# Gated sum of a Fourier mixer and a token MLP: Down's gathers without the gate and two PSUM banks at a time, five Fourier products as seven sub-products, the gate's rows in stage two

## The chip, the cores and the metric

The kernel runs on one core of a Trainium2 chip. The time is device microseconds of one execution. Before the change it is 1871.37 us, the median of 3 runs (1871.29 to 1871.44).

## What is computed

The input is `x` with S = 2048 tokens and D = 1024 channels, all in float32. Two blocks of it are mixed by a gate per token:

```python
a = einsum("bsd,ed->bse", x, dft_hid_re)            # A: a Fourier layer, real part
b = einsum("bsd,ed->bse", x, dft_hid_im)
A = einsum("ts,bse->bte", dft_seq_re, a) - einsum("ts,bse->bte", dft_seq_im, b)

h = layernorm(x)                                    # B: an MLP over the tokens, F = 3584
u = gelu(einsum("bsd,sf->bdf", h, w1) + b1)
B = (einsum("bdf,fs->bds", u, w2) + b2).transpose(0, 2, 1)

g = sigmoid((x * gate_w).sum(-1, keepdims=True))
out = g * A + (1 - g) * B
```

## The kernel before

**Four stages.** Each is one large matrix product, and they run one after the other on TensorE: *Fourier* (names with q; the sequence transform, 2048 x 2048 for the cosine and for the sine, times x, written to DRAM as `q`), *Up* (u; w1 times the normalised rows `h`, then gelu, written as `u`), *Mixed* (y; the hidden transform of `q`, times the gate, into the output) and *Down* (o; w2 times `u`, times one minus the gate, added onto the output).

**26 block products per stage.** A stage is a bilinear scheme (`SCHEME`): the matrices are cut into 4 x 4 by 4 x 2 blocks, and 26 products of sums of blocks give what 32 products of blocks would. For each product VectorE (DVE) adds or subtracts blocks (L606, L609), sums that are used again being kept or stored and loaded again; ScalarE (ACT) then rounds an operand to a high part (L636), DVE makes the low part (L643, or L641 with the sign turned), and TensorE multiplies high x high, high x low and low x high (L948 to L950). A product has 96 matmuls of 128x128 by 128x512 in Fourier (4 row blocks m, 2 column halves n, 4 k), 84 in Up (7 m, 4 k), 48 in Mixed (4 m, 4 k) and 84 in Down (4 m, 7 k). One product of Fourier, number 24 of the scheme, is itself made as seven sub-products of 12 matmuls (`strassen`, L1097), named in `Q_INNER`: sums of its quarters are called s and t, its direct quarters a and b, and it adds up some results inside PSUM (L606 on `ps_q_p`).

**Gathers.** A finished product is read out of PSUM once for each block of the result that it belongs to, by a copy if it is the first (L1008, or in Down L1403 on ACT and L1405 on DVE), else by a fused multiply and add on DVE (L1016). Products that follow each other with nearly the same result blocks are chained: the next goes on accumulating in the same banks, and only differences are read. A block that is complete goes to DRAM (L622); if it returns after a gap of more than `Q_GAP` products it is stored and later loaded again or added by an accumulating DMA (L1268 in Fourier). In Down a block is added onto the output by an accumulating DMA of GpSimd (L1445); the blocks that end in the last product are loaded first and stored by SyncE (SP).

**PSUM.** It is four slots of two banks each (`SLOTS["pp"]`). Fourier, Up and Mixed take a slot for two neighbouring m at once and read both with one instruction of 128x1024 (Up's seventh m alone). Down has `together = False`: it takes single banks, halves of a slot, and a half that comes free beside a used half is given out before a free slot is opened. Down's reads are 128x512 and multiply by the gate of their 128 rows (`hgate` or `ngate`, one column of it per row block).

**Gate.** The row products of x with `gate_w` (L1525, sixteen of 128x1024 on DVE into `zg`) are made where the rows for Up are loaded and normalised, at the end of Fourier and the start of Up. The gate itself is made in Up's product 10.

**Order.** All work is listed as tasks with a due place. `Graph.schedule` plays them through by a table of costs and writes down one fixed order for each engine: DVE, ACT, the DMA queue of SP (loads) and the one of POOL (stores and accumulating DMAs). `RESERVE` and `Store.fits` say how many slots are kept for tasks that are due earlier. The engines follow that order and wait on semaphores.

Of the kernel before, what the change touches and what calls it, by code (L numbers as in the profile page):

```python
# [26 lines left out]
RESERVE = 7  # L27
# [81 lines left out]
Q_ORDER = [5, 14, 23, 3, 7, 11, 21, 22, 18, 24, 6, 17, 0, 13, 9, 8, 19, 15, 12, 2, 20, 25, 1, 16, 10, 4]  # L109
# [31 lines left out]
Q_GAP = 8  # L141
Q_DMA = {}
Q_INNER = (24,)
# [69 lines left out]
SUMS_AT, SUMS_STEP = ("q", 4), 2.5  # L213
SQUARES_AT, SQUARES_STEP = ("q", 12), 2
GATES_AT = "u", 10
H_LEAD, H_EACH = 8, 0.6
# [49 lines left out]
class Buf:  # L266
    def __init__(self, kind, name, t=None, parts=1, dtype=F32):
        self.kind, self.name, self.t, self.parts, self.dtype = kind, name, t, parts, dtype
        self.writer = [None] * parts
        self.readers = [[] for _ in range(parts)]  # L270
        self.taker = None
        self.users, self.opens = set(), False
        self.lane = dtype if kind == "h" else kind


class View:
    def __init__(self, buf, c0, n, part=None):
        self.buf, self.c0, self.n, self.part = buf, c0, n, part

    @property  # L280
    def ap(self):
        return self.buf.t[:, self.c0:self.c0 + self.n]
# [52 lines left out]
class Store:  # L335
# [6 lines left out]
    def pairs(self, ahead, kinds):  # L342
        return sum((max(0, ahead[d] - len(self.part[d])) + 1) // 2 for d in kinds)

    def fits(self, b, ahead):
        if b.kind == "f":
            return len(self.free["f"]) > ahead["f"]
        if b.kind == "h":
            if len(self.part[b.dtype]) > ahead[b.dtype]:
                return True  # L350
            return len(self.free["f"]) + len(self.free["h"]) > ahead["f"] + self.pairs(ahead, (F32, F32R))
        if b.kind == "ps" and len(self.part["ps"]) > ahead["ps"]:
            return True
        return len(self.free["pp"]) > ahead["pp"] + self.pairs(ahead, ("ps",))
# [30 lines left out]
class Graph:  # L385
# [63 lines left out]
    def schedule(self):  # L449
# [25 lines left out]
        def has_slots(t):  # L475
            if not all(b.engine for b in t.behind):
                return False
            for b in t.need:
                if not store.fits(b, {k: min(bisect_left(waiting[k], t), RESERVE) for k in waiting}):
# [3 lines left out]
        def start(t, e):  # L483
# [8 lines left out]
            if t.nbytes:  # L492
# [3 lines left out]
                idle[e] = max(idle[e], lanes[e].pop(0))  # L496
            heapq.heappush(events, idle[e])
# [7 lines left out]
        while events:  # L505
# [13 lines left out]
            if idle["PE"] <= now and at < len(pe) and not left[pe[at]] and has_slots(pe[at]):  # L519
                start(pe[at], "PE")  # L520
                at += 1
            for e, heap in ready.items():
                held = []
                while heap and idle[e] <= now and len(held) < 60:
# [3 lines left out]
                    if has_slots(t):  # L528
# [11 lines left out]
def gated_mix_kernel(  # L540
# [84 lines left out]
    def split(key, v, name, negate=False, pair=False):  # L625

        if pair:
# [82 lines left out]
    class Bilinear:  # L710
# [11 lines left out]
        halved = ()  # L722
        together = True
        ahead = 3

        def __init__(self, name, nk, nm, nn, wn, rn, big, keep, order, extra, perm):
# [19 lines left out]
            self.C, self.PS, self.half = {}, {}, {}  # L746
# [16 lines left out]
            for q in range(8):  # L763
                at = [j for j, r in enumerate(self.reads) if q in dict(r)]
                b = perm[0][q // 2] * 2 + perm[2][q % 2]
                self.ends[b] = [i for i, nxt in zip(at, at[1:] + [999]) if nxt - i > self.gap]
# [20 lines left out]
        def during(self, j, key):  # L787
# [10 lines left out]
            if (self.name, j) == GATES_AT:  # L798
                assert len(self.h) == NS
                gates(key)  # L800
# [46 lines left out]
        def operand(self, x, j, k, key):  # L847
# [34 lines left out]
            v, sv, _ = self.term(x, e, last, j, k, key)  # L882
            return v, s * sv

        def build(self):
            nonlocal step
            factor = [1] * self.chains
            for j in range(len(self.out)):
# [5 lines left out]
                for ks in self.groups(j):  # L894
# [21 lines left out]
                    for k in ks:  # L916
                        parts = {}
                        for x in "RW":
# [9 lines left out]
                            parts[x] = [View(h.buf, h.c0 + at, self.n[x], h.part) for h in pair[u]]  # L928
# [4 lines left out]
        def split(self, x, key, v, j, k, negate):  # L933
            return split(key, v, f"{self.name}_p{j}_{x.lower()}_{self.label(k)}", negate, self.pairs and v.n == H)
# [21 lines left out]

        def banks(self, j):
# [11 lines left out]
        def take(self, key, j, m, n, eps):  # L969

            bank, at = self.PS[j % self.chains, m, n], [(m, n)]
            if bank.buf.kind == "pp":
# [4 lines left out]
            for q, coef in self.reads[j]:  # L977
# [10 lines left out]
                if new and not back:  # L988
# [31 lines left out]
    class Fourier(Bilinear):  # L1020
        wide = Q_WIDE
        behind = Q_BEHIND
        halved = Q_INNER
        gap = Q_GAP
        takes = Q_TAKES

        def __init__(self):
            super().__init__("q", 4, 4, 2, H, D, "R", {"R": 1, "W": 2}, Q_ORDER, Q_SUMS, Q_PERM)

        def by_dma(self, x_, j, k, o):  # L1030
            return x_ == "R" and j > 1 and k in Q_DMA.get(Q_ORDER[j], ())
# [231 lines left out]
        def finish(self, key, b, m, n, o, j):  # L1263
            dst, reg = self.place(b, m, n)
            if j == self.ends[b][0] or self.back(b, j):
# [99 lines left out]
    class Down(Bilinear):  # L1365
# [6 lines left out]
        together = False  # L1372
# [24 lines left out]

        def copy(self, key, b, m, n, o, ps, coef):
# [206 lines left out]
```

## Time and profile before

| | |
|---|---|
| median of 3 runs | 1871.37 us |
| the profiled execution | 1871.47 us, span 1869.7 us |
| granted TensorE clock | 1.000 |
| DMA | 473.20 MB, 253 GB/s; queue of SP 369.19 MB, of POOL 102.26 MB |
| HBM | 367.81 MB read, 103.81 MB written |

Line numbers are those of the kernel before. In the profile's groups stands line, engine, operation, output <- inputs, shape and count, then busy time, mean duration in ns, and the idle time of the engine just before these instructions with what ended it. PE is TensorE, PEld its weight loads, SPq the queue of SP. In the windows each engine has its busy time and, in brackets, its instructions. How the time lies over the stages is read in the prediction.

### The profile page before, as it was taken

To read this page: it belongs to the slowest core of one execution; us is meant where nothing else is said; L and a number is where in the kernel's file an instruction comes from. 1 tells how busy PE (TensorE), PEld (TensorE's weight loads), DVE (VectorE), ACT (ScalarE), POOL (GpSimd) and SP (SyncE) were. 2 spreads that over 40 slices of the span, in tenths; PEclk is the share of its full clock that TensorE was granted. 3 is DMA by queue.
4 is the path that set the end of the run, shared out by engine and by line. 5 is a ranking of instruction groups with operands and counts; after the bars stand their busy time and mean duration, and the time that the engine had idled before them with its cause. 6 is when DMAs were issued, how large, how long until landed. Compare 5 with 4: busy or idle time off the path is not lost.

```text
span 1869.7 us, 23585 instructions
## 1 busy us (share of the span) xinstructions
PE 1848.6 (99%) x8118; PEld 1519.9 (81%) x8118; DVE 1688.5 (90%) x2091; ACT 873.4 (47%) x1210; POOL 200.7 (11%) x346
## 2 busy tenths in 40 slices
PE   9999999999999999999999999999999999999999
PEld 7888888888888888888888888788887778778887
DVE  8899779979979989696979999999999998889995
ACT  5445436643466434343535654454654344444441
POOL 0100010021021120001101200010310010001101
PEclk9999999999999999999999999999999999999999
DMA  9977679889697766366675988587997564675963
GB/s 379 387 262 277 223 279 364 316 293 392 231 326 266 252 231 234 127 231 203 224 251 209 373 280 261 194 273 285 326 338 238 182 207 158 186 203 119 300 178 68
DMA packets 187303, 473.20 MB, mean 253 GB/s; under 512 B 22768, under 2 KB 23536, under 8 KB 187184
## 3 DMA queue, kind: packets, MB, share of 16 engines
q1 hardware_dynamic: 154224, 369.19, 57.4%
q0 software_dynamic: 32672, 102.26, 16.7%
q8 instruction: 63, 1.03, 0.2%
q14 instruction: 56, 0.46, 0.1%
q10 hardware_dynamic: 288, 0.26, 0.0%
HBM read 367.81 MB, written 103.81 MB: 252 GB/s over the span
## 4 chain that ended last, share of the span: by engine, by line
PE 86%; DVE 8%; DMA 3%; issue 1%; ACT 1%; SPq 0%; DVEq 0%; ACTq 0%
PE ps_o_p L948 9%; PE ps_u_p L949 9%; PE ps_u_p L948 9%; PE ps_u_p L950 9%; PE ps_q_p L950 9%; PE ps_q_p L948 9%; PE ps_q_p L949 9%; PE ps_o_p L950 9%; PE ps_o_p L949 9%; PE ps_y_p L948 2%; PE ps_y_p L950 2%; PE ps_y_p L949 2%; DVE y_c L1016 1%; PE ps_q_p L1097 1%; DVE o_c L1016 1%
## 5 line engine op out<-in xcount | busy, mean ns | idle before, releaser
L950 PE MATMUL ps_q_p<-q_p_r_hi,q_p_w_lo 128*128 128x512 f32 x784 | 305.2, 389 | 0.9 <-DVE q_p_w_lo L641 0.8
L949 PE MATMUL ps_q_p<-q_p_r_lo,q_p_w_hi 128*128 128x512 f32 x784 | 305.0, 389 | 0.0
L948 PE MATMUL ps_q_p<-q_p_r_hi,q_p_w_hi 128*128 128x512 f32 x784 | 305.0, 389 | 0.0
L948 PE MATMUL ps_o_p<-o_p_r,o_p_w 128*128 128x512 f32 x726 | 284.7, 392 | 13.3 <-DVE o_c L1016 11.3
L949 PE MATMUL ps_o_p<-o_p_r,o_p_w 128*128 128x512 f32 x726 | 282.6, 389 | 0.0
L950 PE MATMUL ps_o_p<-o_p_r,o_p_w 128*128 128x512 f32 x726 | 282.6, 389 | 0.0
L949 PE MATMUL ps_u_p<-u_p_r_lo,u_p_w_hi 128*128 128x512 f32 x518 | 201.5, 389 | 0.0
L948 PEld LDWEIGHTS ps_o_p<-o_p_r,o_p_w 128*128 128x128 f32 x726 | 136.2, 188 | 49.3 <-DVE o_c L1016 13.1
L636 ACT ACTIVATE q_p_r_hi<-q_R_p 128x1024 fp32r<-128x1024 f32 (+1 forms) x96 | 100.4, 1053 | 160.2 <-DVE q_R_p L606 78.9
L950 PEld LDWEIGHTS ps_q_p<-q_p_r_hi,q_p_w_lo 128*128 128x128 f32 x784 | 147.1, 188 | 32.4 <-DVE q_p_w_lo L641 1.7
L949 PEld LDWEIGHTS ps_q_p<-q_p_r_lo,q_p_w_hi 128*128 128x128 f32 x784 | 147.1, 188 | 30.7
L948 PEld LDWEIGHTS ps_q_p<-q_p_r_hi,q_p_w_hi 128*128 128x128 f32 x784 | 147.2, 188 | 30.2
L950 PEld LDWEIGHTS ps_o_p<-o_p_r,o_p_w 128*128 128x128 f32 x726 | 136.3, 188 | 28.5
L949 PEld LDWEIGHTS ps_o_p<-o_p_r,o_p_w 128*128 128x128 f32 x726 | 136.3, 188 | 27.7
L636 ACT ACTIVATE u_p_w_hi<-u_W_p 128x896 fp32r<-128x896 f32 x104 | 97.4, 949 | 128.1 <-DVE u_W_p L606 68.3
L948 PE MATMUL ps_u_p<-u_p_r_hi,u_p_w_hi 128*128 128x512 f32 x385 | 149.8, 389 | 0.0
L950 PE MATMUL ps_u_p<-u_p_r_hi,u_p_w_lo 128*128 128x512 f32 x385 | 149.8, 389 | 0.0
L948 PE MATMUL ps_u_p<-u_p_r_lo,u_p_w_hi 128*128 128x512 f32 x343 | 133.4, 389 | 0.0
L950 PE MATMUL ps_u_p<-u_p_r_lo,u_p_w_lo 128*128 128x512 f32 x343 | 133.4, 389 | 0.0
L643 DVE TENSOR_TENSOR q_p_r_lo<-q_R_p,q_p_r_hi 128x1024 fp32r<-128x1024 f32 (+1 forms) x96 | 115.5, 1217 | 9.6 <-ACT q_p_r_hi L636 5.9
L1016 DVE SCALAR_TENSOR_TENSOR q_c<-ps_q_p,q_c 128x1024 f32<-128x1024 f32 x84 | 101.1, 1222 | 23.1 <-PE ps_q_p L950 20.2
L949 PEld LDWEIGHTS ps_u_p<-u_p_r_lo,u_p_w_hi 128*128 128x128 f32 x518 | 97.2, 188 | 20.2
(414 smaller groups left out, 3738.9 us busy)
## 6 DMA issues: line engine op xcount, KB each, us to landing
q_R_p<-in_ct_dram SPq DMA_DIRECT2D x131, 512.0 KB, 8.1
u_W_p<-in_w_dram SPq DMA_DIRECT2D x120, 448.0 KB, 5.0
o_W_p<-in_w_dram SPq DMA_DIRECT2D x94, 256.0 KB, 5.3
q<-q_c POOLq DMA_DIRECT2D x80, 256.0 KB, 6.8
q_W_p<-in_x_dram SPq DMA_DIRECT2D x77, 256.0 KB, 8.4
u<-u_c POOLq DMA_DIRECT2D x74, 256.0 KB, 4.5
y_W_p<-q SPq DMA_DIRECT2D x72, 256.0 KB, 5.6
y_R_p<-in_dt_dram SPq DMA_DIRECT2D x53, 256.0 KB, 5.9
```

The lines of the kernel that those rows point to most:

```text
L636: g.add({"ACT": act(v.n)}, key, lambda e: nc.scalar.activation(hi.ap, v.ap, AF.Copy, scale=-1.0 if negate else 1.0), r=(v.reg,), w=(hi.reg,))
L643: nc.vector.tensor_sub(lo.ap, v.ap, hi.ap.bitcast(F32))
L948: nc.tensor.matmul(bank.ap, wh.ap[:, c], rh.ap[:, e], start=a, stop=False, skip_group_check=True)
L949: nc.tensor.matmul(bank.ap, wh.ap[:, c], rl.ap[:, e], start=False, stop=False, skip_group_check=True)
L950: nc.tensor.matmul(bank.ap, wl.ap[:, c], rh.ap[:, e], start=False, stop=b, skip_group_check=True)
L1016: lambda e: nc.vector.scalar_tensor_tensor(o.ap, ps.ap, scale, o.ap, op0=ALU.mult, op1=ALU.add),
L1097: nc.tensor.matmul(bank.ap, l, r, start=start and k == i == 0, stop=done and k == 1 and i == 2, skip_group_check=True)
```

## The change

It does five things.

1. `Q_INNER` names five products of the scheme (1, 4, 15, 17, 24) instead of one: four more products of Fourier are made as seven sub-products.
2. Down takes PSUM in pairs of banks (`together = False` goes) and its copies and fused adds no longer multiply by the gate; a finished block is multiplied once, by ACT, ahead of its accumulating DMA. Blocks that are added onto the loaded output (those that end in the last product) are still read bank by bank, with the gate. In the last product, two banks have a slot each.
3. The row products of the gate leave `normalise` and have loads of their own in Up (`row_gates`, from product 4 on, one row for every three steps); the gate is made behind them.
4. Fourier's tables: other sums are kept (`Q_XR`, `Q_KEEP`), some sums of R blocks are made by an accumulating load (`Q_DMA`), a gap for each block (`Q_GAP`), and a block that returns is always added by an accumulating DMA. `Q_ORDER` swaps two neighbours, and the squares start at product 16.
5. The planner reserves 6 slots instead of 7, and does not let ACT or DVE start on a PSUM slot that the other is still reading.

```diff
-RESERVE = 7
+RESERVE = 6
...
-Q_ORDER = [5, 14, 23, 3, 7, 11, 21, 22, 18, 24, 6, 17, 0, 13, 9, 8, 19, 15, 12, 2, 20, 25, 1, 16, 10, 4]
+Q_ORDER = [5, 14, 23, 3, 7, 11, 21, 22, 18, 24, 6, 17, 0, 13, 9, 8, 19, 15, 12, 2, 25, 20, 1, 16, 10, 4]
...
-Q_GAP = 8
-Q_DMA = {}
-Q_INNER = (24,)
+Q_GAP = (12, 3, 12, 6, 12, 12, 1, 3)
+Q_KEEP = (2, 2)
+Q_INPLACE = ""
...
+Q_DMA = {10: (0, 2, 10), 24: (2, 10), 2: (1, 2), 16: (3, 10, 12), 19: (3, 12), 23: (1, 2, 3), 17: (0, 1, 3, 10, 12), 15: (0, 1), 20: (10,), 21: (3, 10), 13: (0, 2), 0: (3, 12), 3: (0, 2), 22: (10,), 14: (10,), 8: (10, 12), 6: (0,), 9: (1,), 18: (12,), 4: (3,), 5: (0,)}
...
+Q_INNER = (1, 4, 15, 17, 24)
...
-SQUARES_AT, SQUARES_STEP = ("q", 12), 2
-GATES_AT = "u", 10
-H_LEAD, H_EACH = 8, 0.6
+SQUARES_AT = ('q', 16)
+SQUARES_STEP = 2
+GATES_AT = "u", 4
+GATES_STEP = 3
+H_LEAD = 5
+H_EACH = 0.6
...
+            if e != "PE" and any(b.kind in ("ps", "pp") and b.reader not in (None, e) and b.until > now for b in t.bufs):
+                return False
...
             bank, at = self.PS[j % self.chains, m, n], [(m, n)]
-            if bank.buf.kind == "pp":
+            if bank.part is not None:
...
-                if new and not back:
+                if len(at) > 1 and self.single(b, j):
+                    for i, (one, part) in enumerate(zip(at, os)):
+                        self.accumulate(key, b, *one, part, View(bank.buf, i * H, H, i), eps * coef)
+                elif new and not back:
                     self.copy(key, b, m, n, o, bank, eps * coef)
...
-            if j == self.ends[b][0] or self.back(b, j):
+            if j == self.ends[b][0] or (b, m, n) in self.brought:
                 store(key, dst, reg, o)
...
-        together = False
...
+        def single(self, b, j):
+            return self.back(b, j)
+
+        def banks(self, j):
+            super().banks(j)
+            if j == len(self.out) - 1:
+                for m in (2, 3):
+                    self.PS[j % self.chains, m, 0] = View(Buf("pp", f"ps_o_p{j}_{m}_0", None, 4), 0, H)
+
         def copy(self, key, b, m, n, o, ps, coef):
-            i, t = (b // 2) * 4 + m, hgate if coef > 0 else ngate
...
+            plain_copy(key, o, ps, float(coef))
 
         def accumulate(self, key, b, m, n, o, ps, coef):
+            if not self.back(b, self.reading):
+                return fused(key, o, ps, float(coef))
             i, t = (b // 2) * 4 + m, hgate if coef > 0 else ngate
             fused(key, o, ps, t.t[:, i:i + 1], (t,))
...
-                g.add({"POOL": ISSUE["POOL"]}, key, lambda e: nc.gpsimd.dma_start(dst, o.ap, accum_op=ALU.add),
+                g.add({"ACT": act(H) + 0.08}, key, lambda e: nc.scalar.activation(
+                    o.ap, o.ap, AF.Copy, scale=hgate.t[:, i:i + 1]), r=(o.reg, hgate), w=(o.reg,))
+                g.add({"POOL": ISSUE["POOL"]}, key + 0.5, lambda e: nc.gpsimd.dma_start(dst, o.ap, accum_op=ALU.add),
...
-    def normalise(k, v, key):
-
-        col, junk = slice(k, k + 1), slot(D, f"z{k}")
+    def row_gates(k, key):
+        v, col = slot(D, f"x{k}_g"), slice(k, k + 1)
+        if GW.buf.taker is None:
+            load(key, GW, bass.AP(tensor=gate_w.tensor, offset=gate_w.offset, ap=[[0, P], [1, D]]))
         load(key, v, x[k * P:(k + 1) * P, :])
...
-            junk.ap, v.ap, 1.0, GW.ap, op0=ALU.mult, op1=ALU.mult, accum_out=zg.t[:, col]),
+            v.ap, v.ap, 1.0, GW.ap, op0=ALU.mult, op1=ALU.mult, accum_out=zg.t[:, col]),
```

How this moves instructions shows at three places.

The first is PE in Down, at the end of the sixth product (p5, its last k) and the start of the seventh (p6). A PSUM slot is named by the tile that opened it: `ps_o_p4_2_0` is the slot of banks m = 2 and 3, opened by the fifth product and still used by the chained sixth. Before:

```order
L949 MATMUL ps_o_p4_2_0_11532<-o_p5_r_6_11567,o_p5_w_6_11573 128x512
L950 MATMUL ps_o_p4_2_0_11532<-o_p5_r_6_11567,o_p5_w_6_11573 128x512
L948 MATMUL ps_o_p4_2_0_11532<-o_p6_r_0_11596,o_p6_w_0_11561 128x512
L949 MATMUL ps_o_p4_2_0_11532<-o_p6_r_0_11596,o_p6_w_0_11561 128x512
L950 MATMUL ps_o_p4_2_0_11532<-o_p6_r_0_11596,o_p6_w_0_11561 128x512
```

And the same place now:

```order
L974 MATMUL ps_o_p4_2_0_11687<-o_p5_r_6_11716,o_p5_w_6_11722 128x512
L975 MATMUL ps_o_p4_2_0_11687<-o_p5_r_6_11716,o_p5_w_6_11722 128x512
L973 MATMUL ps_o_p6_0_0_11977<-o_p6_r_0_11747,o_p6_w_0_11725 128x512
L974 MATMUL ps_o_p6_0_0_11977<-o_p6_r_0_11747,o_p6_w_0_11725 128x512
L975 MATMUL ps_o_p6_0_0_11977<-o_p6_r_0_11747,o_p6_w_0_11725 128x512
```

Before, the seventh product's first bank is a half of the slot that the sixth product has just left; now it is in a slot opened for it.

The second is DVE at the same boundary, where it reads the sixth product into a block (`o_c5`). Before:

```order
L1016 SCALAR_TENSOR_TENSOR o_c5_0_10966<-ps_o_p4_0_0_11509,ngate_77,o_c5_0_10966 128x512
L641 SCALAR_TENSOR_TENSOR o_p7_w_2_11787<-o_W11_p2_0_10818,o_p7_w_2_11787 128x512
L1016 SCALAR_TENSOR_TENSOR o_c5_0_10966<-ps_o_p4_0_0_11509,ngate_77,o_c5_0_10966 128x512
L609 TENSOR_TENSOR o_W3_p1_5_10766<-o_W3_p1_5_10766,o_R2_p1_1_10570 128x512
L1016 SCALAR_TENSOR_TENSOR o_c5_2_10991<-ps_o_p4_2_0_11532,ngate_77,o_c5_2_10991 128x512
L609 TENSOR_TENSOR o_R3_p0_6_10513<-o_R3_p0_6_10513,y_W0_p3_0_8416 128x512
L1016 SCALAR_TENSOR_TENSOR o_c5_2_10991<-ps_o_p4_2_0_11532,ngate_77,o_c5_2_10991 128x512
```

Now:

```order
L1048 SCALAR_TENSOR_TENSOR o_c5_0_11143<-ps_o_p4_0_0_11663,o_c5_0_11143 128x1024
L622 TENSOR_TENSOR u_Rs16_1_7835<-u_Rs16_1_7835,o_R2_p1_2_10789 128x512
L622 TENSOR_TENSOR o_W11_p2_0_10985<-o_W11_p2_0_10985,y_R4_p4_1_8660 128x512
L1048 SCALAR_TENSOR_TENSOR o_c5_2_11166<-ps_o_p4_2_0_11687,o_c5_2_11166 128x1024
L661 TENSOR_TENSOR o_p7_r_3_11989<-u_c1_6_5307,o_p7_r_3_11989 128x512
```

Four reads of one bank with the gate became two of two banks without it.

The third is DVE in Fourier at the twelfth product (p11; number 17 of the scheme), one of the four that change their form. Before, it makes the low parts of the operands while it reads an earlier product:

```order
L643 TENSOR_TENSOR q_p11_w_0_1_lo_2003<-q_W7_p10_0_1_1791,q_p11_w_0_1_hi_1918 128x1024
L643 TENSOR_TENSOR q_p11_r_0_lo_2014<-q_R28_p10_0_1718,q_p11_r_0_hi_2001 128x1024
L643 TENSOR_TENSOR q_p11_r_1_lo_2026<-q_R28_p10_1_1772,q_p11_r_1_hi_2011 128x1024
L606 TENSOR_TENSOR q_R28_p10_2_1855<-q_R28_p10_2_1855,q_R11_p11_2_1940 128x1024
L1016 SCALAR_TENSOR_TENSOR q_c1_0_1094<-ps_q_p9_0_0_1814,q_c1_0_1094 128x1024
L606 TENSOR_TENSOR q_R28_p10_3_1871<-q_R28_p10_3_1871,q_R11_p11_3_1943 128x1024
L643 TENSOR_TENSOR q_p11_r_2_lo_2060<-q_R28_p10_2_1855,q_p11_r_2_hi_2051 128x1024
```

Now the sums t and s, their splits and the sums inside PSUM stand there (ten rows of it):

```order
L625 TENSOR_TENSOR q_p11_t3_2174<-q_R28_p10_2_1638,q_R9_p9_0_1476 128x512
L625 TENSOR_TENSOR q_p11_t3_2174<-q_R28_p10_3_1724,q_R28_p10_1_1553 128x512
L625 TENSOR_TENSOR q_p11_s3_2181<-q_W7_p10_0_1_1567 128x512
L1042 TENSOR_SCALAR q_p11_p5_2193<-ps_q_p11_2_1_2155 128x1024
L661 TENSOR_TENSOR q_p11_t3_lo_2208<-q_p11_t3_2174,q_p11_t3_hi_2189 128x1024
L661 TENSOR_TENSOR q_p11_s3_lo_2219<-q_p11_s3_2181,q_p11_s4_hi_2179 128x512
L622 TENSOR_TENSOR ps_q_p11_0_1_2221<-ps_q_p11_2_0_2127,q_p11_p5_2193 128x1024
L661 TENSOR_TENSOR q_p11_s3_lo_2219<-q_p11_s_1992,q_p11_s4_hi_2179 128x512
L661 TENSOR_TENSOR q_p11_t4_lo_2236<-q_p11_t_1931,q_p11_t4_hi_2166 128x1024
L1048 SCALAR_TENSOR_TENSOR q_c5_0_402<-ps_q_p11_0_0_2162,q_c5_0_402 128x1024
```

Short sums and splits of 128x512 took the place of splits of 128x1024, and they stand among the product's own reads. Over the whole program PE has 8080 matmuls instead of 8128, DVE 2099 instructions instead of 2077.

90 lines of the change are left out of this document (54 added, 36 removed).

## Prediction

> **What bounds the kernel now.** I read the page's head and its chain first, to see which engine carries the span.
>
> ```profile
> span 1869.7 us, 23585 instructions
> PE 1848.6 (99%) x8118; PEld 1519.9 (81%) x8118; DVE 1688.5 (90%) x2091; ACT 873.4 (47%) x1210; POOL 200.7 (11%) x346
> PEclk9999999999999999999999999999999999999999
> PE 86%; DVE 8%; DMA 3%; issue 1%; ACT 1%; SPq 0%; DVEq 0%; ACTq 0%
> ```
>
> TensorE is 99% busy at full clock and has 86% of the chain, so time is won in two ways only: fewer matmuls, or fewer gaps between them. A matmul's record overlaps the next one, so its price is not the mean of a group but the distance between starts. The chain of waits has one piece that gives it:
>
> ```profile
> 202.11 19.04 PE ps_q_p L1097 x84
> ```
>
> 84 matmuls in 19.04 us without a break: 0.2267 us each. This piece is also the one block product of Fourier that is already made as seven sub-products. Next, the gaps stage by stage, from the first matmul of each stage in the timeline of PE:
>
> ```profile
> 4.03 0.80 PE L1241 MATMUL ps_q_p<-q_p_r_hi,q_p_w_hi 128*128 128x256 f32 x2
> 569.58 0.39 PE L948 MATMUL ps_u_p<-u_p_r_hi,u_p_w_hi 128*128 128x512 f32 x1
> 1064.62 0.39 PE L948 MATMUL ps_y_p<-y_p_r,y_p_w 128*128 128x512 f32 x1
> 1350.87 0.39 PE L948 MATMUL ps_o_p<-o_p_r,o_p_w 128*128 128x512 f32 x1
> 1863.55 1.59 PE L1432 MATMUL ps_o_p<-o_p_r,o_p_w 128*128 128x256 f32 x12
> ```
>
> The program has 25 x 96 + 84 = 2484 matmuls of full width in Fourier, 26 x 84 = 2184 in Up, 26 x 48 = 1248 in Mixed and 26 x 84 - 6 = 2178 in Down before the last line. At 0.2267 us these are 563.0, 495.0, 282.9 and 493.7 us. The stages took 565.6, 495.0, 286.3 and 512.7. **Lost between matmuls: 2.5 in Fourier, 0 in Up, 3.4 in Mixed, 19.0 in Down.** The groups of the page agree on whom the stage waits for (their idle column is smaller, since an ending record covers 0.16 us of each gap):
>
> ```profile
> L948 PE MATMUL ps_o_p<-o_p_r,o_p_w 128*128 128x512 f32 x726 | 284.7, 392 | 13.3 <-DVE o_c L1016 11.3
> L948 PE MATMUL ps_y_p<-y_p_r,y_p_w 128*128 128x512 f32 x208 | 81.7, 393 | 1.5 <-DVE y_c L1016 1.4
> ```
>
> In Down it is the read of a PSUM bank by L1016. One such place, after the sixth product, in the timelines of PE, ACT and DVE:
>
> ```profile
> 1467.72 0.39 PE L950 MATMUL ps_o_p<-o_p_r,o_p_w 128*128 128x512 f32 x1
> 1468.21 0.69 ACT L1403 ACTIVATE o_c<-ps_o_p,hgate 128x512 f32<-128x512 f32 x1 [0.52 <-PE ps_o_p L950]
> 1468.99 0.74 DVE L1016 SCALAR_TENSOR_TENSOR o_c<-ps_o_p,ngate,o_c 128x512 f32<-128x512 f32 x1
> 1469.79 0.50 PE L948 MATMUL ps_o_p<-o_p_r,o_p_w 128*128 128x512 f32 x1 [1.67 <-DVE o_c L1016]
> 1471.05 0.40 PE L950 MATMUL ps_o_p<-o_p_r,o_p_w 128*128 128x512 f32 x1
> 1471.48 0.69 ACT L1403 ACTIVATE o_c<-ps_o_p,hgate 128x512 f32<-128x512 f32 x1 [2.58 <-PE ps_o_p L950]
> 1472.20 0.75 DVE L1016 SCALAR_TENSOR_TENSOR o_c<-ps_o_p,ngate,o_c 128x512 f32<-128x512 f32 x1 [1.87 <-ACT o_c L1403]
> 1473.01 0.50 PE L948 MATMUL ps_o_p<-o_p_r,o_p_w 128*128 128x512 f32 x1 [1.57 <-DVE o_c L1016]
> ```
>
> Six matmuls run between two waits of 1.84 and 1.73 us (the distances 2.07 and 1.96, less 0.23). By the order of PE (the first place shown with the change) these six are the first bank of the next product, and it lies in the slot whose two banks ACT and DVE are just reading: it waits for the read of the old half, and the read at 1471.48 in turn waits until the six are done. Mixed, which takes its banks two at a time and so whole slots, loses 3.4 us over as many products.
>
> **The change, part by part.** *Matmuls.* Four more products of Fourier go from 96 to 84: 48 x 0.2267 = **10.9 us** off PE. The other stages keep their counts.
>
> *Down's banks.* Banks are taken in pairs, each in a slot of its own; in the order the seventh product starts in another slot than the one being read. What remains is a chained product, which goes on in the same banks: its first pair is complete when the second pair's 12 matmuls (2.72 us) begin, and these are what the reads have to fit behind.
>
> ```profile
> 1172.05 2.28 DVE y_c L1016 x2
> L1016 DVE SCALAR_TENSOR_TENSOR o_c<-ps_o_p,ngate,o_c 128x512 f32<-128x512 f32 x52 | 38.9, 749 | 24.6 <-PE ps_o_p L950 21.5 <-ACT o_c L1403 2.7
> ```
>
> Two reads of a pair are 2.28 us on DVE, under 2.72, so even a pair read twice is free just in time. Mixed does exactly this over as many products, with DVE fuller than Down's: its 3.4 us is the nearest row, and I take it. **Down: 19.0 to 3.4, 15.6 us off**; the ends are 0 left and 19.0 left. The gate now comes once per finished block, 28 times, on ACT (like the next row), which is idle more than half of the stage, and the accumulating DMA behind it has a whole product of 19 us; cost 0. Without that cover each would put 0.8 us before a DMA whose block nothing in Down reads again.
>
> ```profile
> L1307 ACT ACTIVATE y_c<-y_c,biases,gate 128x512 f32<-128x512 f32 x32 | 23.8, 807 | 18.1 <-DVE y_c L1016 18.0
> ```
>
> *DVE in Fourier.* Seven sub-products need sums and splits of their own. Counted in the order of DVE, Fourier gets 76 more instructions of 128x512 (32 for t, 16 for s, 20 folded splits, 8 of b) and 9 fewer of 128x1024 (16 + 8 splits, 15 sums of R and 8 reads go; 16 + 8 + 4 splits, 8 sums and 2 copies in PSUM come). Back to back they cost 0.60 and 1.14:
>
> ```profile
> 1201.00 1.20 DVE y_p_w L641 x2
> 1202.20 1.14 DVE y_R_p L606
> core 0: us, PE busy (x) PEld busy (x) DVE busy (x) ACT busy (x) POOL busy (x), PEclk, DMA share, GB/s
> 0.00:569.00 569.00, 567.33 (x2494) 467.52 (x2495) 501.05 (x477) 281.55 (x326) 56.66 (x104) 1.00 0.85 312
> 569.00:1064.00 495.00, 495.00 (x2186) 409.87 (x2185) 436.51 (x510) 226.90 (x305) 63.99 (x119) 1.00 0.67 230
> 1064.00:1350.00 286.00, 284.47 (x1249) 233.23 (x1248) 283.63 (x350) 149.37 (x208) 32.35 (x61) 1.00 0.80 273
> 1350.00:1870.00 520.00, 501.83 (x2195) 409.26 (x2193) 467.31 (x757) 215.56 (x373) 47.73 (x63) 1.00 0.67 200
> 400.00:500.00 100.00, 100.00 (x443) 82.77 (x442) 95.36 (x93) 38.66 (x41) 10.72 (x20) 1.00 0.82 312
> 0.00:569.00 569.00, 14.52 (x24) 1.00 0.85 312
> ```
>
> That is 76 x 0.60 - 9 x 1.14 = 35.3 us more. The gate's 16 row products (L1525, the last row, 14.52 us of them in this stage) go to Up. So DVE has 501 + 35 - 15 = 521 of 558 us, 93%. The window 400 to 500 shows DVE at 95% and PE without a gap, and the sub-products at 202 had none; Mixed, with DVE at 99%, lost 3.4 in 286, which over 558 us would be 6.6. I take 1 us, with the ends 0 and 6.6. Up gets the 15 us and reaches 451 of 495, below the same window: 0.
>
> *Gate rows.* Their loads (16 of 512 KB, with the gate's row) join Up, where DMA is at 0.67 of its time and PE never waits; one more ACT table load there. SP's queue issues 1058 DMAs in all instead of 1073, so nothing is pushed back on it. Cost 0, and if Up's cover were gone some 1.3 us for the table.
>
> *DMA in Fourier.* 112 stores of q instead of 80, 48 of them accumulating instead of 8; 15 loads of R add onto a tile by DMA; 8 reloads of q, and some of R, go. The bytes stay near 312 x 569 = 177 MB; the accumulated part is 48 x 0.26 + 15 x 0.52 = 20.4 MB. What an accumulated byte costs the engines no row says outright; the eight of before land in 9.0 us at the median, all stores of q in 6.8:
>
> ```profile
> L1268 POOL DMA_DIRECT2D q<-q_c x8: 855/1040/1218, 519.6 to 528.3; - x8
> DMA to landing us min/median/max: 3.8/9.0/12.0
> q<-q_c POOLq DMA_DIRECT2D x80, 256.0 KB, 6.8
> 0.00:100.00 100.00, 98.45 (x427) 79.60 (x428) 85.95 (x78) 52.17 (x54) 7.87 (x18) 1.00 1.00 381
> ```
>
> At 9.0/6.8 = 1.3 the stage would need 183 MB in 558 us, 328 GB/s; the first 100 us ran at 381 with DMA full, and PE lost little. I take 0; the upper end is the rival below. On POOL the accumulating issues take 1.0 us, and 56.7 of 569 us were busy there, so its queue has room.
>
> **Sum** against the profiled execution: 1869.7 - 10.9 - 15.6 + 1 = 1844.2 of span. That execution took 1871.47, 1.8 more than its span, and lies 0.1 above the median of the runs, so 1846.0 is the forecast.
>
> **Rivals.** *(a) Pairs wait as long as single banks.* A pair can be read only when both banks are done, and holds both until the last reader is through. If DVE arrives late at each of the places with two reads per pair, the 19.0 us stay: 1846.0 + 15.6 = 1861.6. There are eight such places; at the two waits seen above, 3.6 us each, they would even make 29, and 1871.6, no change. For it: DVE reads in order and other instructions stand ahead of a read. Against it: Mixed. [...]
>
> *(b) DMA bounds Fourier.* If an accumulated byte counts three times, the stage carries 177 + 41 = 218 MB, at 381 GB/s 572 us instead of 558: 14 us lost, 1860. For it: DMA share 0.85 already. Against: landings only 1.3 times as long.
>
> *(c) The same, worse, and slower than before.* Fourier's DMA decides once it needs 25.4 + 558 = 584 us, that is 222 MB at 381 GB/s, or 3.2 for each accumulated byte. At 3.5 it is 177 + 51 = 228 MB, 598 us, 40 lost: 1885. Only the 12.0 us of the longest landing hints at it.
>
> **Chances.** Forecast (1839 to 1856) 0.78; (a) 0.09 at 1861.6 and 0.03 at no change; (b) 0.07; (c) 0.03. A measurement of this kernel tells about 0.2% (3.7 us) from no change. So faster 0.94, same 0.03, slower 0.03. Low end: nothing left in Down and 1 us less in Fourier, 1846.0 - 3.4 - 1 = 1841.6, and up to 2 us fewer in Mixed, 1839.5. High end: 6.6 of DVE in Fourier gives 1851.6, and the range reaches to (b): 1860.
>
> **What would show it.** Right: five pieces of 84 matmuls on L1097's successor at 19.04 us each; from the first matmul of Down to its last line about 497 us; the idle of the ps_o group at 2 us or less; DVE in Fourier near 520 us. Wrong: PE waiting in Fourier for DVE splits or for DMA landings of R (b, c), or ps_o still waiting for o_c reads of 1.2 us (a).

## The result and the profile after

The changed kernel takes **1841.34 us** (median of 4 runs, 1840.95 to 1843.12); the kernel before took 1871.4 beside it. The ratio is 0.984 with a 95% interval of 0.9823 to 0.9857. The profiled execution took 1840.95 us. Its page begins so, and its chain of waits has these shares:

```profile
span 1839.2 us, 23662 instructions
PE 1832.2 (100%) x8070; PEld 1512.4 (82%) x8070; DVE 1710.5 (93%) x2113; ACT 923.8 (50%) x1284; POOL 244.0 (13%) x389
PEclk9999999999999999999999999999999999999999
PE 87%; DVE 8%; DMA 3%; issue 1%; ACT 0%; SPq 0%; DVEq 0%; ACTq 0%
```

There are 48 matmuls fewer, 22 us more of VectorE, and the clock is full. The first matmuls of the stages and of the last line, in the timeline of PE:

```profile
4.08 0.58 PE L1274 MATMUL ps_q_p<-q_p_r_hi,q_p_w_hi 128*128 128x256 f32 x1
559.66 0.39 PE L973 MATMUL ps_u_p<-q_p_s_lo,u_p_w_hi 128*128 128x512 f32 x1
1054.70 0.39 PE L973 MATMUL ps_y_p<-y_p_r,y_p_w 128*128 128x512 f32 x1
1338.92 0.39 PE L973 MATMUL ps_o_p<-o_p_r,o_p_w 128*128 128x512 f32 x1
1833.76 0.28 PE L1471 MATMUL ps_o_p<-o_p_r,o_p_w 128*128 128x256 f32 x1
```

Fourier has 2436 matmuls now, the others what they had. With the prediction's 0.2267 us for each, the stages of 555.6, 495.0, 284.2 and 494.8 us **lost 3.4, 0, 1.3 and 1.1 us** between matmuls (before: 2.5, 0, 3.4 and 19.0). The 30.5 us by which the span fell are thus 10.9 of matmuls, 17.9 of waits in Down, 2.1 in Mixed and 0.7 behind the last line, less 0.9 that Fourier lost more (each rounded). The groups of PE agree:

```profile
L973 PE MATMUL ps_o_p<-o_p_r,o_p_w 128*128 128x512 f32 x726 | 283.0, 390 | 0.2 <-DVE o_c L1048 0.2
L973 PE MATMUL ps_y_p<-y_p_r,y_p_w 128*128 128x512 f32 x208 | 81.4, 391 | 0.3 <-DVE y_c L1048 0.3
```

The start of Down's seventh product, where the kernel before waited 1.84 and 1.73 us, in the timelines of PE, ACT and DVE. The first two rows are the end of one product and the start of the next, 0.22 us apart; the reads of the old banks go on behind that start, and nobody waits for them, since the new product has another slot:

```profile
1453.12 0.39 PE L975 MATMUL ps_o_p<-o_p_r,o_p_w 128*128 128x512 f32 x1
1453.34 0.39 PE L973 MATMUL ps_o_p<-o_p_r,o_p_w 128*128 128x512 f32 x1
1453.60 1.03 ACT L1040 ACTIVATE o_c<-ps_o_p 128x1024 f32<-128x1024 f32 x1 [1.69 <-PE ps_o_p L975]
1454.66 1.22 DVE L1048 SCALAR_TENSOR_TENSOR o_c<-ps_o_p,o_c 128x1024 f32<-128x1024 f32 x1
```

The chain has four of the five sub-product blocks as single pieces:

```profile
201.71 19.04 PE ps_q_p L1130 x84
371.90 19.04 PE ps_q_p L1130 x84
477.98 19.04 PE ps_q_p L1130 x84
540.54 19.29 PE ps_q_p L1130 x84
```

The fifth, from 242.3 us on, takes 19.04 us as well; the chain runs over transfers there.

### The profile page after: what moved, and what is told of

It is laid out like the page before. It is cut to its first block, busy times and chain, and to the rows that moved or that the text cites. A ratio compares the mean times of both kernels' runs of the same rounds, so it can differ in the third digit from the quotient of the medians.

```text
span 1839.2 us, 23662 instructions
## 1 busy us (share of the span) xinstructions
PE 1832.2 (100%) x8070; PEld 1512.4 (82%) x8070; DVE 1710.5 (93%) x2113; ACT 923.8 (50%) x1284; POOL 244.0 (13%) x389
## 4 chain that ended last, share of the span: by engine, by line
PE 87%; DVE 8%; DMA 3%; issue 1%; ACT 0%; SPq 0%; DVEq 0%; ACTq 0%
PE ps_u_p L973 9%; PE ps_u_p L974 9%; PE ps_u_p L975 9%; PE ps_o_p L973 9%; PE ps_o_p L974 9%; PE ps_o_p L975 9%; PE ps_q_p L975 7%; PE ps_q_p L974 7%; PE ps_q_p L973 7%; PE ps_q_p L1130 4%; PE ps_y_p L973 3%; PE ps_y_p L974 3%; PE ps_y_p L975 3%; DMA q_W_p<-in_x_dram 1%; DVE y_c L1048 1%
## 5 line engine op out<-in xcount | busy, mean ns | idle before, releaser
L974 PE MATMUL ps_q_p<-q_p_r_lo,q_p_w_hi 128*128 128x512 f32 x656 | 255.3, 389 | 1.3 <-DVE q_p_r_lo L661 1.3
L975 PE MATMUL ps_q_p<-q_p_r_hi,q_p_w_lo 128*128 128x512 f32 x656 | 255.3, 389 | 0.6 <-DVE q_p_w_lo L659 0.6
L973 PE MATMUL ps_q_p<-q_p_r_hi,q_p_w_hi 128*128 128x512 f32 x656 | 255.2, 389 | 0.0
L974 PE MATMUL ps_u_p<-u_p_r_lo,u_p_w_hi 128*128 128x512 f32 x609 | 236.9, 389 | 0.0
L973 PE MATMUL ps_u_p<-u_p_r_lo,u_p_w_hi 128*128 128x512 f32 x420 | 163.4, 389 | 0.0
L975 PE MATMUL ps_u_p<-u_p_r_lo,u_p_w_lo 128*128 128x512 f32 x420 | 163.4, 389 | 0.0
L974 PEld LDWEIGHTS ps_q_p<-q_p_r_lo,q_p_w_hi 128*128 128x128 f32 x656 | 123.1, 188 | 27.0 <-DVE q_p_r_lo L661 1.7
L975 PEld LDWEIGHTS ps_q_p<-q_p_r_hi,q_p_w_lo 128*128 128x128 f32 x656 | 123.1, 188 | 26.7 <-DVE q_p_w_lo L659 1.0
L973 PEld LDWEIGHTS ps_q_p<-q_p_r_hi,q_p_w_hi 128*128 128x128 f32 x656 | 123.1, 188 | 25.5
L1048 DVE SCALAR_TENSOR_TENSOR u_c<-ps_u_p,u_c 128x1024 f32<-128x1024 f32 (+1 forms) x83 | 94.3, 1164 | 9.4 <-PE ps_u_p L975 9.4
L622 DVE TENSOR_TENSOR q_R_p<-q_R_p,q_R_p 128x1024 f32<-128x1024 f32 x69 | 82.4, 1216 | 13.2 <-DMA q_R_p<-in_ct_dram 13.1
```

The source lines that it names most:

```text
L622: g.add({"DVE": dve(o.n)}, key, lambda e: nc.vector.tensor_add(o.ap, a.ap, b.ap), r=(a.reg, b.reg), w=(o.reg,))
L973: nc.tensor.matmul(bank.ap, wh.ap[:, c], rh.ap[:, e], start=a, stop=False, skip_group_check=True)
L974: nc.tensor.matmul(bank.ap, wh.ap[:, c], rl.ap[:, e], start=False, stop=False, skip_group_check=True)
L975: nc.tensor.matmul(bank.ap, wl.ap[:, c], rh.ap[:, e], start=False, stop=b, skip_group_check=True)
L1048: lambda e: nc.vector.scalar_tensor_tensor(o.ap, ps.ap, scale, o.ap, op0=ALU.mult, op1=ALU.add),
```

## The experiments

Each kernel is the changed one with the edit shown. "Lost" is worked out as above, from each kernel's own timeline of PE and its own number of matmuls (12 fewer for each more sub-product block). The ratio is to the kernel before. DVE is VectorE's busy time in the whole span, from the page. The losses are those of one profiled execution of each kernel. Every edit makes the planner lay out the whole program anew, so a stage that an edit doesn't touch moves too: Fourier loses 3.4 to 4.9 us in the kernels that differ in Down alone, and Down 1.0 to 1.5 us in most of those that leave it alone. Differences of 1.5 us in Fourier and of 0.5 in Down show nothing by themselves. Products are counted from 0, so that the seventh is product 6.

| kernel | us (median) | ratio, 95% interval | lost: Fourier | Up | Mixed | Down | DVE |
|---|---|---|---|---|---|---|---|
| before | 1871.4 | 1 | 2.5 | 0 | 3.4 | 19.0 | 1688.5 |
| changed | 1841.34 | 0.984 (0.9823-0.9857) | 3.4 | 0 | 1.3 | 1.1 | 1710.5 |
| gated_single_reads | 1844.8 | 0.9857 (0.984-0.9873) | 4.9 | 0 | 1.4 | 3.2 | 1721.1 |
| single_reads | 1843.25 | 0.9849 (0.9834-0.9863) | 4.1 | 0 | 1.4 | 2.6 | 1715.8 |
| half_slots | 1850.75 | 0.9887 (0.9872-0.9902) | 4.4 | 0 | 1.4 | 9.6 | 1713.8 |
| half_slots_gated | 1853.58 | 0.9903 (0.9888-0.9918) | 4.4 | 0 | 1.4 | 12.7 | 1718.7 |
| one_inner | 1850.93 | 0.989 (0.9875-0.9904) | 2.3 | 0.3 | 1.6 | 1.0 | 1641.5 |
| six_inner | 1850.23 | 0.9891 (0.9874-0.9907) | 12.5 | 1.4 | 1.4 | 1.5 | 1723.4 |
| six_inner_early | 1850.18 | 0.9885 (0.987-0.9899) | 14.7 | 0 | 1.4 | 1.1 | 1723.7 |
| seven_inner | 1862.97 | 0.9954 (0.9939-0.9969) | 30.3 | 1.4 | 1.4 | 1.5 | 1740.2 |
| gate_rows_early | 1856.2 | 0.9917 (0.99-0.9934) | 5.4 | 12.1 | 2.1 | 1.5 | 1712.0 |
| r_sums_on_dve | 1844.88 | 0.9856 (0.9842-0.9871) | 3.5 | 2.5 | 2.1 | 1.4 | 1737.1 |
| gap8 | 1853.09 | 0.99 (0.9885-0.9914) | 11.9 | 1.7 | 1.6 | 1.0 | 1721.5 |
| no_reader_rule | 1849.2 | 0.9878 (0.9864-0.9893) | 8.9 | 0 | 2.9 | 2.5 | 1714.1 |

### Down: the slots, the joined reads or the gate?

**gated_single_reads** reads bank by bank, with the gate, and drops ScalarE's scaling:

```diff
         def single(self, b, j):
-            return self.back(b, j)
+            return True
...
         def accumulate(self, key, b, m, n, o, ps, coef):
-            if not self.back(b, self.reading):
-                return fused(key, o, ps, float(coef))
             i, t = (b // 2) * 4 + m, hgate if coef > 0 else ngate
```

> The changed kernel, whose Down products keep slots in pairs of their own, but the slots are read one bank at a time and with the gate, as before, and nothing is scaled by ScalarE ahead of the stores: of the three edits of Down only the slots are left. Theory (the 19 us were lost because a product that opens its banks got halves of the slot that was still being read, so the slots alone remove the loss): Down loses 1 to 3 us between its matmuls, and the time is 1841 to 1844 us. Rival (the joined reads, or reads without the gate's column, made VectorE and ScalarE quick enough): the loss comes back, 10 to 19 us in Down, and the time is 1850 to 1860 us.

Measured 1844.8 us, Down lost 3.2, though the reads are those of the kernel before. From there it is 15.8 us less, but the plan around Down differs as well; what the slots alone are worth, half_slots_gated tells below. The time is 0.8 above the expected range since Fourier lost 1.5 us more, at waits of its own. The rival falls.

**single_reads** keeps reads without the gate and parts the joined reads alone (the hunk on `single` above, and not the second).

> The changed kernel with slots in pairs and reads without the gate, but each of Down's banks read by an instruction of its own; this leaves out the joined reads alone. Theory (slots decide): Down loses 1 to 3 us, the time is 1841 to 1844 us. VectorE's and ScalarE's busy time in Down grows, since an instruction's fixed cost is paid twice, but both have room there. Rival (joining the reads is what shortened the waits): 10 us or more lost in Down, 1850 us or more.

Measured 1843.25 us, Down lost 2.6. The fixed cost shows from 1338 to 1840 us: VectorE is busy 462.8 us instead of 457.2, ScalarE 229.6 instead of 227.1. In the changed kernel's Down a read of 128x1024 that adds takes 1.218 us on VectorE and one of 128x512 (with the gate) 0.746, so two short ones take 0.27 more. Joining the reads is worth 1.5 us of waits in Down (2.6 to 1.1). Reading without the gate takes 0.6 (3.2 to 2.6), which is hardly more than the scatter.

**half_slots** goes the other way: one line, and the banks are halves of slots again.

```diff
         ahead = O_AHEAD
+        together = False
```

> The changed kernel with Down's banks given out singly again, as halves of slots, and so read one at a time; the reads stay without the gate and ScalarE scales before the stores, as in the changed kernel. Theory (shared slots cost the time): the loss comes back where an unchained product starts in the slot that the product before it leaves, which by the order of instructions is so for products 3, 9, 12, 15 and 22, at 1 to 3.6 us each: Down loses 6 to 19 us and the time is 1847 to 1860 us. Rival (the gate's removal from the reads is what counts): Down loses under 3 us, and the time stays at 1841 to 1844 us.

Measured 1850.75 us, Down lost 9.6. The longest waits of PE stand where products 3, 9, 15 and 22 start, at 0.85 to 1.3 us for each read waited for; product 12 waited less than 0.2 us, so four of the five places were right. Against single_reads, which differs in the slots alone, the halves cost 7.0 us (2.6 to 9.6).

**half_slots_gated** has the edits of gated_single_reads and of half_slots together: Down as it was before, in the changed plan.

> The changed kernel with the whole of Down as before: banks as halves of slots, read one at a time with the gate's column, and no scaling by ScalarE. What differs from the kernel before, in Down, is which half each bank was given. By the list of slots, a product that opens its banks does so in the slot that the product ahead of it still has read at 3, 4, 6, 9, 15 and 16 (six; before at nine or ten, and with halves but without the gate at 3, 9, 12, 15 and 22, five, where 9.6 us were lost). Theory (the loss goes by the number of such starts, some 1.9 us each): Down loses 10 to 14 us, at these six places and nowhere else much, and the time is 1850.5 to 1855 us. Rival (reads with the gate make up the other half of the loss): 17 to 20 us lost, 1858 to 1861 us.

Measured 1853.58 us, Down lost 12.7, and PE waits 0.5 to 1.1 us at the starts of 3, 4, 6, 9, 15 and 16, as expected; the only other wait above 0.4 us in Down is one of 0.57. The start of product 16, in the timeline of PE and DVE with the same pattern as before: a read, the matmuls that waited for it, the next read, the next wait.

```profile
1654.11 0.39 PE L975 MATMUL ps_o_p<-o_p_r,o_p_w 128*128 128x512 f32 x1
1654.54 0.75 DVE L1049 SCALAR_TENSOR_TENSOR o_c<-ps_o_p,hgate,o_c 128x512 f32<-128x512 f32 x1
1655.43 0.47 PE L973 MATMUL ps_o_p<-o_p_r,o_p_w 128*128 128x512 f32 x1 [0.94 <-DVE o_c L1049]
1657.10 0.75 DVE L1049 SCALAR_TENSOR_TENSOR o_c<-ps_o_p,hgate,o_c 128x512 f32<-128x512 f32 x1 [1.22 <-PE ps_o_p L975]
1657.91 0.51 PE L973 MATMUL ps_o_p<-o_p_r,o_p_w 128*128 128x512 f32 x1 [0.84 <-DVE o_c L1049]
```

So the waits stand where a product opens its banks in the slot that is being read, and nowhere else of weight. The rival falls here too: reads with the gate make the loss 3.1 us larger (9.6 to 12.7, at six starts instead of five), not double. Against gated_single_reads, which differs in the slots alone, **halves cost 9.5 us (3.2 to 12.7)**.

The kernel before, with the same reads and halves in Down, lost 6.3 us more. The number of starts doesn't explain that: in its trace PE waits over 0.4 us only at the starts of 2, 3, 6, 9, 12, 15 and 16. Products 6 and 12 alone cost 7.1 us there, by two waits of 1.7 to 1.8 us each; here product 6 costs 0.5 and product 12 nothing. At both places of the kernel before, ScalarE and VectorE read one after the other (the prediction shows product 6). The planner's rule on readers (below), which it lacked, and the other halves that the banks got aren't parted.

### Do the matmuls come through?

```diff
-Q_INNER = (1, 4, 15, 17, 24)
+Q_INNER = (24,)
```

> The changed kernel with one block product as seven sub-products instead of five, so 48 matmuls more in Fourier, and the block sums for the four others not made. Theory (VectorE's added work was hidden, the matmuls come through at 0.2267 us each): Fourier is 10 to 11 us longer, the time is 1851 to 1852.5 us. If lateness of VectorE or of transfers had eaten part of the gain, Fourier's loss of 3.4 us falls as well and the time is below 1850 us; the loss can fall by at most 3.4 us, which bounds this from below at 1848.8 us.

Measured 1850.93 us, just under the expected range and 9.6 more than the changed kernel, for 48 x 0.2267 = 10.9 us of matmuls. Fourier's loss fell from 3.4 to 2.3. VectorE's busy time fell by 69.0 us: **the four blocks bring 69 us of VectorE with them, and all of it costs TensorE about 1 us**, no more than the scatter.

### How much more does VectorE hide in Fourier?

Three kernels add sub-product blocks: six_inner, seven_inner and six_inner_early, in this order.

```diff
-Q_INNER = (1, 4, 15, 17, 24)
+Q_INNER = (1, 4, 12, 15, 17, 24)
...
+Q_INNER = (1, 4, 9, 12, 15, 17, 24)
...
+Q_INNER = (1, 3, 4, 15, 17, 24)
```

> The changed kernel with a sixth block product (12) as seven sub-products: 12 matmuls fewer, -2.7 us, for some 6 us more of VectorE in Fourier, whose share there goes from 92 to about 94%. Theory (VectorE still hides): 1838 to 1839.5 us. Rival (VectorE is at its limit at 92%): every us of VectorE added comes out in Fourier, 1843 to 1846 us.

> The changed kernel with two more block products (9 and 12) as seven sub-products: 24 matmuls fewer, -5.4 us, for some 13.6 us more of VectorE, 527 of some 552 us in Fourier (95 to 96%). Theory: most of it still hides, but the lateness at single places grows, 1836 to 1840 us, below six sub-product blocks or level with them. Rival (VectorE bounds Fourier): 1845 us or more.

> The changed kernel with a sixth block product as seven sub-products, but the fourth of the order (3) instead of the nineteenth (12), whose VectorE work of some 14 us falls into the first 100 us, where VectorE is busy 73 of 100 us, and not right behind another such block; 12 matmuls fewer. Theory (VectorE's load at the place decides, not its mean over the stage): Fourier loses under 6 us, 1838.5 to 1841 us. Rival (the mean decides, 95% being too much): Fourier loses 10 us or more, 1845 us or more.

Measured 1850.23, 1862.97 and 1850.18 us: all three theories miss, and far; the times are those of the rivals, for the first even longer. The blocks were also priced too low: VectorE's busy time grew by 12.9, 29.7 and 13.2 us. Set beside that the time lost against the changed kernel, with the saved matmuls (2.7, 5.4, 2.7) put back: 11.6, 27.0 and 11.5 us. So the time lost is nearly as large as the VectorE time added. Part of it is the clock's: behind waits the granted clock fell to 0.50 (last section), for 6.8 us in six_inner, 13.7 in seven_inner and 3.4 in six_inner_early. With matmuls 0.43 us apart instead of 0.2267, as six_inner shows them there, that can account for about half of these times by estimate, 3.4, 6.8 and 1.7 us.

The loss stands where VectorE is full. Windows of 50 us, of the changed kernel, six_inner and seven_inner (busy time of PE, PEld, DVE, ACT and POOL, with instructions; granted clock; DMA share; GB/s):

```profile
400.00:450.00 50.00, 50.00 (x223) 41.40 (x222) 49.18 (x44) 23.68 (x31) 11.34 (x16) 1.00 1.01 339
400.00:450.00 50.00, 45.19 (x186) 35.73 (x185) 50.00 (x47) 29.70 (x42) 11.34 (x16) 0.93 0.90 321
300.00:350.00 50.00, 45.76 (x193) 35.40 (x192) 50.00 (x51) 25.29 (x29) 9.26 (x12) 1.00 0.79 240
```

A full VectorE isn't enough, though: from 100 to 150 us it is busy 49.98 of 50 us in the changed kernel, and PE loses nothing.

six_inner_early doesn't decide between the place and the mean. Its block was to fall where VectorE had room, but VectorE's busy time in the first 100 us rose by 3.0 us only (72.6 to 75.6), and from 80 to 140 us it was full; there PE lost, with one wait of 2.76 us at 88.4 us into the run.

Three more take from VectorE's room or give to it. **gate_rows_early** puts the gate's rows back, and makes the gate in Up's product 10 as before:

```diff
             if (self.name, j) == GATES_AT:
-                for row in range(NS):
-                    row_gates(row, key + GATES_STEP * row)
-                gates(key + GATES_STEP * NS)
+                gates(key)
...
     def normalise(k, v, key):
+        col, junk = slice(k, k + 1), slot(D, f"z{k}")
         load(key, v, x[k * P:(k + 1) * P, :])
+        g.add({"DVE": dve(D)}, key, lambda e: nc.vector.scalar_tensor_tensor(
+            junk.ap, v.ap, 1.0, GW.ap, op0=ALU.mult, op1=ALU.mult, accum_out=zg.t[:, col]),
+            r=(v.reg, GW.reg), w=(junk.reg, zg))
```

> The changed kernel with the gate's sixteen row products made where before made them, with each row that is normalised, so that some 14.5 us of VectorE go back from Up to the end of Fourier. Theory (VectorE is full in Fourier after the first 100 us, so what comes on top of it comes out of TensorE's time one for one, as with the sixth sub-product block): Fourier loses 12 to 18 us instead of 3.4, and the time is 1850 to 1856 us. Rival (VectorE at 95% on the average still hides, and the sixth block failed only for following upon another such block): Fourier loses under 6 us, 1841 to 1844 us.

Measured 1856.2 us, 14.9 more. The size is that of the theory (0.2 above its range), the place is not: Fourier loses 5.4, and Up, which starts with its operands late, 12.1. Half of the sixteen row products run after Up's start, and the clock is at 0.50 for 13.7 us there, which can account for up to 6.8 us. Its first matmuls in the timeline of PE, with the wait of each in brackets:

```profile
561.67 0.50 PE L971 MATMUL ps_u_p<-u_p_r_hi,u_p_w_hi 128*128 128x512 f32 x1 [2.16 <-ACT u_p_r_hi L654]
564.92 0.80 PE L972 MATMUL ps_u_p<-u_p_r_hi,u_p_w_hi 128*128 128x512 f32 x1 [2.75 <-DVE u_p_r_hi L661]
```

**gap8** restores the one gap, so that blocks of q are held longer and stored less:

```diff
-Q_GAP = (12, 3, 12, 6, 12, 12, 1, 3)
+Q_GAP = 8
```

> The changed kernel with the old rule for when a block of q is stored and opened anew (a gap of 8 products for all blocks), so 16 accumulating stores of q instead of 48; the reads that open a block anew become reads that add to it. Theory (accumulating stores cost the stage next to nothing): within 2 us of the changed kernel, save that blocks held longer take tiles from the splits, up to 1846 us, and the wait of 1.4 us near 294 us into the run stays. Rival (accumulating stores hold up the loads): that wait goes and Fourier loses under 2 us, 1839 to 1840 us.

Measured 1853.09 us, 11.8 more; both expectations miss. A reason stands in the groups that read q's banks in Fourier, first of the changed kernel and then of gap8:

```profile
L1048 DVE SCALAR_TENSOR_TENSOR q_c<-ps_q_p,q_c 128x1024 f32<-128x1024 f32 x76 | 90.7, 1215 | 2.9 <-PE ps_q_p L975 2.4 <-PE ps_q_p L1130 0.2
L1040 ACT ACTIVATE q_c<-ps_q_p 128x1024 f32<-128x1024 f32 x48 | 48.3, 1024 | 39.8 <-PE ps_q_p L975 39.6
```

```profile
L1048 DVE SCALAR_TENSOR_TENSOR q_c<-ps_q_p,q_c 128x1024 f32<-128x1024 f32 x90 | 106.9, 1217 | 3.7 <-PE ps_q_p L975 2.9 <-ACT q_c L1040 0.5
L1040 ACT ACTIVATE q_c<-ps_q_p 128x1024 f32<-128x1024 f32 x34 | 34.4, 1025 | 36.4 <-PE ps_q_p L975 36.4
```

A block opened anew is read by a plain copy, which ScalarE makes here in 1.02 us; a block held is read by an add, which in these kernels VectorE alone makes, in 1.22 us. Fourteen reads change engine, and VectorE's busy time grows by 11.0 us. On balance the accumulating stores are thus no price of the change but a way to give VectorE's work to ScalarE and the DMA. That blocks held longer also take tiles from the splits, as the expectation says, isn't parted from it.

**r_sums_on_dve** makes all sums of R on VectorE:

```diff
-Q_DMA = {10: (0, 2, 10), 24: (2, 10), 2: (1, 2),
...
+Q_DMA = {}
```

> The changed kernel with the sums of R all made by VectorE instead of by loads that add onto a tile. VectorE in Fourier grows by some 14 us, and the transfers shrink by as many accumulating loads. Theory (VectorE binds, the transfers don't): Fourier loses 10 to 18 us, 1848 to 1856 us. Rival (late transfers make up Fourier's 3.4 us): the loss falls to 2 us or less and the time to 1839 to 1841 us.

Measured 1844.88 us, 3.5 more, though VectorE is 26.6 us busier in the span, 19.3 of them before 558 us: both expectations miss, and so would a price of one for one. Fourier's length is the same to 0.1 us; 2.5 us are lost in Up. The windows of the first 100 us and of the rest of Fourier up to 558 (columns as above), of the changed kernel, of r_sums_on_dve, and the second one of one_inner, show how full VectorE is in each:

```profile
0.00:100.00 100.00, 98.63 (x429) 79.88 (x429) 72.64 (x67) 51.81 (x55) 12.23 (x23) 1.00 1.01 370
100.00:558.00 458.00, 456.75 (x2014) 377.69 (x2013) 440.68 (x446) 265.71 (x325) 83.67 (x122) 1.00 0.90 300
```

```profile
0.00:100.00 100.00, 98.52 (x426) 79.39 (x427) 84.70 (x77) 52.59 (x55) 7.90 (x18) 1.00 1.00 377
100.00:558.00 458.00, 457.54 (x2017) 378.08 (x2016) 447.93 (x450) 259.60 (x319) 74.25 (x112) 1.00 0.86 300
```

```profile
100.00:558.00 458.00, 458.00 (x2022) 379.53 (x2021) 372.22 (x347) 239.02 (x285) 82.02 (x121) 1.00 0.91 303
```

Twelve of r_sums_on_dve's us fall into the first 100, where VectorE has room. After that VectorE goes from 440.7 to 447.9 of 458, and PE is busy for 457.5 of them, no less than in the changed kernel. six_inner has less of VectorE in the same stretch, 445.6 us, and PE only 451.8: the mean over the stage doesn't decide. Why these sums fit where a sixth block or the gate's rows did not isn't settled; the sums of R may be due earlier than splits and be made ahead, but no run parts that.

### The planner's rule on readers

```diff
-            if e != "PE" and any(b.kind in ("ps", "pp") and b.reader not in (None, e) and b.until > now for b in t.bufs):
-                return False
```

> The changed kernel without the planner's new rule that VectorE or ScalarE doesn't start on a PSUM slot while the planner has the other of them on it. Theory (the rule is what took 2 us from Mixed): Mixed loses 2.5 to 4 us again instead of 1.3, the rest stays, and the time is 1842.5 to 1845 us. Rival (Mixed gained from other shifts of the plan, as of the gate's rows leaving it): Mixed stays at 1 to 2 us, and the time at 1840.5 to 1842.5 us.

Measured 1849.2 us, 7.9 more. Mixed loses 2.9 as the theory had it, but Down 2.5 and Fourier 8.9, which neither had. Fourier's groups of VectorE show the cost: 12.7 us in which VectorE, in its fixed order, stood before a PSUM slot that ScalarE was reading. In the changed kernel no such wait of Fourier is listed.

```profile
L1046 DVE SCALAR_TENSOR_TENSOR q_c<-ps_q_p,q_c 128x1024 f32<-128x1024 f32 x73 | 87.8, 1224 | 11.1 <-ACT q_c L1038 7.2 <-PE ps_q_p L973 2.4 <-PE ps_q_p L1128 1.5
L1040 DVE TENSOR_SCALAR q_c<-ps_q_p 128x1024 f32<-128x1024 f32 x11 | 13.4, 1222 | 6.1 <-ACT q_c L1038 5.5 <-PE ps_q_p L973 0.5
```

None of the twelve is faster than the changed kernel.

## Why the prediction was right, point by point

**Matmuls, 10.9 us: right.** Taking four of the five blocks back costs 9.6 us, of which 10.9 are matmuls and about -1 is Fourier's smaller loss.

**Down, 19.0 to 3.4: the mechanism was right, the term too small.** It measured 17.9 us instead of 15.6; 1.1 are left. Step by step (19.0, 12.7, 3.2, 2.6, 1.1), 6.3 of the 17.9 go with the new plan already while the banks are still halves; own slots are worth 9.5, reads without the gate 0.6, and joined reads 1.5. The slots are shown from both sides: with them Down loses 3.2 us at most, whatever the reads, and without them 9.6 to 12.7, nearly all at the places that the slots give. The 3.4 was taken from Mixed of the kernel before as the nearest row. That row was itself about to change: in Mixed of the kernel before, VectorE's reads of y waited 2.2 us for ScalarE's, and 2.1 in no_reader_rule; in the changed kernel, with the planner's rule, no such wait is listed there. Without the rule Down loses 2.5 and Mixed 2.9.

**Mixed 0: it was 2.1 us faster.** The rule on readers was described with the change, and the sum doesn't price it; the low end allows 2 us fewer in Mixed without a reason. 1.6 of the 2.1 us go when the rule goes. The 2.3 us of Down, these 2.1 and 0.7 behind the last line are the 5 us by which the span came out below the sum's 1844.2.

**VectorE in Fourier, 1 us: right in size, with part of the reasons.** The count gave 20 us more VectorE in the stage. It is 14 more: 514.9 us up to 559.6, against 501.1 up to 569 before. The instructions of Fourier were counted rightly; that ten fewer of Up's stand there was not. TensorE lost 0.9 us more. But "93% of Fourier" says little: after 100 us VectorE is busy 440.7 of 458 us, 96%, and in five of six kernels that added 11 to 30 us of it, or moved 14.5 into the end of the stage, TensorE lost about as much, part of it by the clock. The gate's rows, costed at 0 in Up, were worth 14.9 us by leaving the end of Fourier and the start of Up. The accumulating stores, of which the prediction asked only what they cost the DMA, carried fourteen of VectorE's reads away. And without the rule on readers the term would have been 6.4 us, at the end of its range. That it came out at 0.9 is in part luck: the 1 us was taken between two ends, without the rule, and kernels that differ in Down alone scatter by 1.5.

**DMA in Fourier 0: holds as far as tried.** With 32 accumulating stores fewer (gap8) or without the accumulating loads (r_sums_on_dve) Fourier loses no less. In both VectorE's work grew at the same time, so what the transfers cost by themselves isn't parted. Rivals (b) and (c), which had 14 and 40 us lost in Fourier, fall by the 3.4 that it lost.

**Rival (a)** supposed that pairs wait as long as single banks. The reads of 1.2 us stand behind a start that does not wait for them, and the joined reads leave 1.1 us in Down where the same slots read singly leave 2.6. Reading the banks singly took 1843.25 against 1841.34 us.

## What to carry to other kernels

A bank that is given out should not share a slot with one that is still being read, which cost Down 7.0 and 9.5 us here: list which slot each group opens in, and the places of the waits can be named before a run (here four of five, and six of six). Judge an engine's room by windows of its fullest stretch, not by the stage's mean; here 69 us of VectorE were hidden almost free and the next 13 cost 12, part of it by the clock. When an edit is priced by the nearest row, ask whether another edit of the same change alters that row.

## What the runs showed of the hardware

**Behind some waits of TensorE of about 2 us the granted clock stood at 0.50 for 3.4 us or more.** In six_inner PE waited 1.33 us, ran two matmuls, and waited 1.94 us; soon the matmuls started 0.43 us apart instead of 0.2267, and the granted clock of the window behind is 0.50:

```profile
408.00:413.00 5.00, 2.92 (x12) 1.86 (x10) 5.00 (x6) 4.83 (x6) 0.00 (x0) 0.97 1.03 419
413.00:418.00 5.00, 4.14 (x9) 2.93 (x10) 5.00 (x5) 2.57 (x6) 1.07 (x2) 0.50 1.03 410
```

So it was after single waits of 2.04 us in no_reader_rule and 2.08 in gap8, and not after one of 2.03 in gated_single_reads, nor after the one of 1.41 in the changed kernel (294 us into the run, clock 1.00 there). The length alone doesn't decide: one of 2.28 us in six_inner, beginning at 418.2 us, was followed by the full clock. The trace has 3.41 us at 0.50 in no_reader_rule and gap8 (mean granted clock of the run 0.999), and 6.83 in six_inner (0.998); in each of the first two, seven matmuls 0.43 us apart add 1.4 us to the wait.

**An accumulating load lands as soon as a plain one here, an accumulating store later.** In the changed kernel the loads of R that add onto a tile (issued by GpSimd) land after 8.7 us at the median and the plain ones (by SP) after 8.8; the accumulating stores of q (L1301) after 10.5 and the plain ones (L638) after 6.7.
